# Attention with pooled keys, then a soft mixture of experts, in one planned program: the row sums' epsilon moves to ScalarE, the output gets rows of 4 KB, the groups are all of eight tiles, and the plan's places change

## The chip, the cores and the metric

The kernel runs on one core of a Trainium2 chip. The metric is the device time of one execution in microseconds (us). TensorE multiplies, VectorE and ScalarE do arithmetic and move results, GpSimd does arithmetic on the side, and SyncE issues most of the DMAs. In the profile these are PE (PEld for its weight loads), DVE, ACT, POOL and SP.

## The reference

```python
# attention: B=4, N=12288 queries, C=128; kv of 384 x 32 positions, pooled 4 x 4 to 768 keys
kv_pool = kv.reshape(B, H // r, r, W // r, r, C).mean(axis=(2, 4))
k = v = kv_pool.reshape(B, -1, C) @ w_sr
s = (q @ k.transpose(0, 2, 1)) / sqrt(C)
a = softmax(s)                       # with 1e-9 in the denominator
x = (a @ v).reshape(B * N, C)
# soft mixture: 8 experts of 4 slots, 32 slots in all
logits = x @ phi
d = exp(logits - logits.max(0)); d /= d.sum(0) + 1e-9      # over all rows
slot_out = relu(slot_input @ w1[e]) @ w2[e]                # slot_input = d.T @ x
c = exp(logits - logits.max(1)); c /= c.sum(1) + 1e-9      # over the 32 slots of a row
return c @ slot_out
```

All tensors are float32.

## The kernel before

The 49152 rows are worked on as 384 tiles of 128 queries, 96 tiles to a batch. The attention's output x is never made: since logits = a @ (v @ phi), the pooled keys times `w_sr @ phi` (called U, 32 columns) stand in for the values, and the slots' inputs are gathered over the keys first and multiplied by the values (V) once per batch.

The program has three parts.

**Head.** The first batch's kv is loaded in eight pieces of 768 KB (`kv_load0`, two halves of four pieces), added up on VectorE (`kv_pool0`, L239 to L242) and multiplied into the keys kT (`kv_k_mm` L263, `kv_k_hi` L266, `kv_k_lo` L270), U (`kv_u_mm` L278 and the steps to `kv_u_lo` L315) and V. The other batches' kv comes during the loop; GpSimd adds it up (L252).

**Loop over the tiles.** For each tile: `qk` (L353, six matmuls of the query's high and low part, which `q_hi` L340 on ScalarE and `q_lo` L343 on GpSimd split) writes the scores into one of three slots; `top` (L357, VectorE) finds the row maximum, `exp` (L369, ScalarE) the exponentials p; `hi` (L376, ScalarE) and `lo` (L379, GpSimd) split four of p's six blocks into two 16-bit halves, which a transposing DMA (`turn` L384) turns; the other two blocks are turned by TensorE (`tp` L391) and taken over by VectorE (`tev` L395). For each group of tiles: `lmm` (L411) makes the logits, `lt_out` (L432, ScalarE) and `lt_turn` (L436, TensorE) turn them back, `recip` (L444, L446) and `rcopy` (L506) prepare the softmax's sums, `logits` (L461) scales, `colmax` to `newmax` (L469 to L486) keep the running column maximum, `below`, `weights` and `scaled` (L490, L498, L511) make the weights d, `ymm` (L532, 64 matmuls for eight tiles) and `yacc` (L542) gather the slots' inputs in `acc`. `rowmax`, `rowsub` (GpSimd, L551), `rowexp` (L554) and `rownorm` (L559 to L561) make the row softmax c in the tensor LL and its reciprocal sums in RM. `lt_turn` and `rcopy` write the same PSUM bank, L; whichever stands later in the program waits for the other. At a batch's end come `yturn`, `slots` (L570, TensorE), `total` (L515 to L520) and `sacc` (L584, L585). There are 47 groups of eight tiles and two of four at the end.

**Tail.** The expert weights are loaded into buffers that the loop leaves; `t_sm` (L826), `t_h` (L842), `t_relu`, `t_ht`, `t_ho`, `t_o` (L867), `t_so`, `t_q` (L885, psq) and `t_shi`/`t_slo` make the slots' outputs shl. `k_mul` (L901, GpSimd) scales c. Then, in 24 chunks of 16 tiles: `c_t` (L908) turns c, `c_hi` (L913, ScalarE) and `c_lo` (L918, VectorE) split it, `o_mm` (L929, po) multiplies, `o_ev` (L936 on ScalarE, L938 on VectorE) takes the halves over, and `o_dma` (L942) writes each half, 512 KB.

Nothing is written in the order in which it runs. The class `Plan` takes all operations with an estimated cost, what they depend on, the buffers that they take and a priority, plays the program through, and emits an operation when its engine would take it: of those that could start within 0.12 us of the earliest, the one with the lowest priority number. A tile's or group's number is its due time plus an offset of the table `LATE`, by operation and, for the tiles' operations, by the place in the group. Each engine then runs its own instructions strictly in the emitted order.

Of the kernel before, what the change touches and what calls it, by code (L numbers as in the profile page):

```python
# [9 lines left out]
F32 = mybir.dt.float32  # L10
# [9 lines left out]
P = 128  # L20
# [99 lines left out]
def attention_then_soft_moe(ctx: ExitStack, tc: tile.TileContext, qT, kv0, kvT, w_sr, w_srT, phi, w1, w2, outT):  # L120
# [58 lines left out]
    nc.vector.memset(ones, 1.0)  # L179
    sel1 = cp.tile([P, NS], F32, tag="sel1", name="sel1")  # L180
# [50 lines left out]

    def kv_load0(h, c):
        t = kvs[h, c] = ring("p32", [P, 2, NK], F32, f"kv0_{h}_{c}").rearrange("p a b -> p (a b)")
        o = (h * R2 + c * KVC) * HK
        nc.sync.dma_start(out=t, in_=kv0[:, o : o + KVC * HK])

    def kv_pool0(h, c):
        a, v = kvs[h, 0], kvs[h, c]
        nc.vector.tensor_tensor(out=a, in0=a, in1=v, op=ALU.add)  # L239
        if c == R2 // KVC - 1:  # L240
            nc.vector.tensor_tensor(out=a[:, : 2 * HK], in0=a[:, : 2 * HK], in1=a[:, 2 * HK :], op=ALU.add)
            nc.vector.tensor_tensor(  # L242
                out=pooled[0][:, h * HK : (h + 1) * HK], in0=a[:, :HK], in1=a[:, HK : 2 * HK], op=ALU.add
            )
# [311 lines left out]
    def rownorm(g):  # L556
        s, n = groups[g]
        r = RM[:, s : s + n]
        nc.vector.tensor_reduce(out=r, in_=ll(g), axis=X, op=ALU.add)  # L559
        nc.vector.tensor_scalar_add(r, r, EPS)  # L560
        nc.vector.reciprocal(out=r, in_=r)  # L561
# [35 lines left out]
    def pool(n):  # L597
# [57 lines left out]
    def kv_ops(b, base, step, dep):  # L655
# [12 lines left out]
        p = base + step * 2  # L668
        d = dep if b else [ops["pool", 1], ops["wo"]]
# [20 lines left out]
    kv_v_ops(0, T(2), [ops["pool", 1], ops["wo"], ops["u", 0]])  # L690

    def group_ops(g):
# [46 lines left out]
        ops["c", g] = go("ks", "DVE", (0.33 * n / GMAX + 0.35, 0.1), [re_], lambda: rownorm(g))  # L739
        if (s + n) % TPB == 0:  # L740
# [4 lines left out]
            fd = go("fd", "ACT", (0.19, 0.1), [ops["nm", g], ops["to", b - 1]], lambda: fade(b, g)) if b else None  # L745
# [305 lines left out]
```

## Time and profile before

| | |
|---|---|
| timed runs | 977.13, 983.35, 1013.5 us; median 983.35 |
| profiled execution | 979.63 us; span 977.8 us |
| busy share of the span | PE 89%, DVE 82%, ACT 74%, POOL 70% |
| read and written in HBM | 58.87 MB and 25.17 MB |
| DMA packets | 452434, of them 408784 under 512 B |

The span goes from the first to the last instruction of the profiled execution. A row of the groups gives line, engine, operation, output and inputs, sizes and count, then busy time and the mean duration, then the engine's idle time before it and who ended most of it. A row of the stretches gives the busy time of PE, PEld, DVE, ACT and POOL with the number of instructions, then the granted clock of TensorE as a share of full speed, the share of the DMA engines and GB/s. A row of the timeline gives start and duration in us, engine, line, operation, and in brackets the idle time before it and what ended it.

### The profile page before, as it was taken

How to read it: one execution, taken by the hardware profiler on the slowest of the kernel's cores; microseconds unless marked ns; L12 is line 12 of the kernel's file. 1: busy time of each engine (PE TensorE's matmuls, PEld its weight loads, DVE VectorE, ACT ScalarE, POOL GpSimd, SP SyncE). 2: the span in 40 equal slices, each digit the busy share in tenths (PEclk: the TensorE clock that was granted, in tenths of full speed). 3: DMA queues.
4: the chain of work that ended last, by engine and by line, in shares of the span. 5: the costliest groups of instructions: out<-in, count | busy, mean ns of one | idle time of the engine just before them, and what ended most of it. 6: DMA issues, size and time to landing. Idle time of an engine off the chain costs nothing. (4 is left out here: it accounts for less than half of the span.)

```text
span 977.8 us, 26937 instructions
## 1 busy us (share of the span) xinstructions
PE 872.0 (89%) x10104; PEld 742.7 (76%) x10104; DVE 798.4 (82%) x1939; ACT 727.4 (74%) x1531; POOL 688.8 (70%) x584
## 2 busy tenths in 40 slices
PE   0898989999999979999998999999999999977871
PEld 0777878888888868888887989888898989753440
DVE  6687888888989898888888888889898989774761
ACT  1697868988887868887887888878888888731650
POOL 1498979776778978867688998767768787683000
PEclk9999989999999989999999999999999999987775
DMA  8499999997899998988899999888989898892999
GB/s 317 86 230 198 210 211 169 164 165 139 148 209 208 217 215 131 176 157 142 156 229 187 214 218 188 157 149 143 167 148 155 171 168 150 137 324 79 339 341 318
DMA packets 452434, 186.47 MB, mean 191 GB/s; under 512 B 408784, under 2 KB 433616, under 8 KB 452304
## 3 DMA queue, kind: packets, MB, share of 16 engines
q1 hardware_dynamic: 451728, 184.35, 92.0%
q8 instruction: 79, 1.29, 0.6%
q14 instruction: 51, 0.42, 0.2%
q10 hardware_dynamic: 576, 0.41, 0.1%
HBM read 58.87 MB, written 25.17 MB: 86 GB/s over the span
## 5 line engine op out<-in xcount | busy, mean ns | idle before, releaser
L379 POOL TENSOR_TENSOR hl<-p,hl 128x512 f16<-128x512 f32 x384 | 440.9, 1166 | 151.1 <-ACT hl L376 140.1
L353 PE MATMUL s<-kT,qs 128*128 128x384 f32 x2304 | 487.7, 352 | 6.8 <-ACT p L369 6.2
L369 ACT ACTIVATE p<-s,nm 128x768 f32<-128x768 f32 x384 | 343.9, 897 | 105.5 <-DVE nm L357 88.8
L353 PEld LDWEIGHTS s<-kT,qs 128*128 128x128 f32 x2304 | 393.0, 191 | 22.2 <-ACT p L369 18.4
L357 DVE CUSTOM_DVE_ANT_1 junk<-s,lnpk 128x768 bf16<-128x768 f32 x384 | 364.9, 950 | 26.3 <-PE s L353 10.5
L376 ACT ACTIVATE hl<-p 128x512 f16<-128x512 f32 x384 | 231.1, 626 | 7.2 <-DMA pt<-hl 3.7
L343 POOL TENSOR_TENSOR qs<-q,qs 128x512 fp32r<-128x512 f32 x96 | 123.5, 1286 | 42.3 <-ACT qs L340 31.5
L532 PE MATMUL DB<-p,dp 128*32 128x192 f32 x3040 | 135.1, 328 | 4.2 <-DVE pf L395 3.5
L395 DVE COPY pf<-DB 128x512 f32<-128x512 f32 x192 | 131.5, 685 | 4.3 <-PE DB L391 3.3
L391 PE MATMUL DB<-ident,p 128*128 128x128 f32 x768 | 117.2, 275 | 4.2 <-DVE pf L395 1.6
L532 PEld LDWEIGHTS DB<-p,dp 128*32 128x32 f32 x3040 | 96.8, 110 | 30.1 <-DVE pf L395 8.4
L391 PEld LDWEIGHTS DB<-ident,p 128*128 128x128 f32 x768 | 94.2, 141 | 15.3 <-ACT p L369 2.3
L411 PE MATMUL L<-pt,u 128*32 128x256 f16 (+1 forms) x2352 | 72.7, 271 | 3.2 <-DMA pt<-hl 3.0
L369 ACT ACTIVATION_READ_ACCUMULATOR p<-s,nm 128x1 f32 x384 | 75.0, 195 | 0.0
L411 PEld LDWEIGHTS <-u 128*32 128x32 f16 x2352 | 63.8, 97 | 12.6 <-DMA pt<-hl 3.8
L252 POOL TENSOR_TENSOR LL<-LL 128x1536 f32<-128x1536 f32 x21 | 73.2, 3486 | 0.0
L340 ACT ACTIVATE qs<-q 128x512 fp32r<-128x512 f32 x96 | 59.9, 624 | 10.5 <-DMA q<-qT 8.8
L542 DVE SCALAR_TENSOR_TENSOR acc<-acc,al,DB 128x192 f32<-128x192 f32 x44 | 18.1, 412 | 44.8 <-PE DB L532 44.8
L411 PE MATMUL L<-pf,us 128*32 128x256 f32 (+1 forms) x784 | 51.5, 380 | 2.2 <-DVE dp L511 2.0
L929 PE MATMUL po<-c,shl 32*128 32x512 f32 x288 | 37.1, 554 | 11.2 <-ACT o L936 7.5
L560 DVE TENSOR_SCALAR RM<-RM 128x8 f32<-128x8 f32 (+1 forms) x49 | 45.6, 930 | 1.7
L938 DVE COPY o<-po 128x1024 f32<-128x1024 f32 x24 | 29.3, 1221 | 19.5 <-DMA outT<-o 12.2
(135 smaller groups left out, 699.1 us busy)
## 6 DMA issues: line engine op xcount, KB each, us to landing
outT<-o SPq DMA_DIRECT2D x48, 512.0 KB, 7.5
q<-qT SPq DMA_DIRECT2D x95, 256.0 KB, 3.2
LL<-kvT SPq DMA_DIRECT2D x24, 768.0 KB, 5.1
kv<-kv SPq DMA_DIRECT2D x8, 768.0 KB, 9.6
pt<-hl SPq DMA_TRANSPOSE x384, 3.5
w<-w SPq DMA_DIRECT2D x7, 768.0 KB, 8.4
w<-w SPq DMA_DIRECT2D x11, 256.0 KB, 6.4
q<-qT ACTq DMA_DIRECT2D x1, 256.0 KB, 9.2
```

The source lines that it names most:

```text
L252: nc.gpsimd.tensor_tensor(out=stage[:, 2:4, :], in0=stage[:, 2:4, :], in1=stage[:, 0:2, :], op=ALU.add)
L340: nc.scalar.activation(QSP[i][:, 0], QS[i], AF.Copy)
L343: nc.gpsimd.tensor_tensor(out=QSP[i][:, 1], in0=QS[i], in1=QSP[i][:, 0].bitcast(F32), op=ALU.subtract)
L353: nc.tensor.matmul(s[:, h, :HK], a, k[:, m, h * HK : (h + 1) * HK], start=(n == 0), stop=(n == 2))
L357: nc.vector.tensor_tensor_reduce(out=junk.rearrange("p (h k) -> p h k", h=2), in0=S[i][:, :, :HK], in1=lnpk.unsqueeze(2).broadcast_to([P, ...
L369: nc.scalar.activation(P32[i // 2][:, i % 2, :].rearrange("p (h k) -> p h k", h=2), S.pop(i)[:, :, :HK], AF.Exp, bias=NM.pop(i), scale=1.0 ...
L376: nc.scalar.activation(HL[i][:, 0], P32[i // 2][:, i % 2, : KD * P], AF.Copy)
L379: nc.gpsimd.tensor_tensor(out=HL[i][:, 1], in0=P32[i // 2][:, i % 2, : KD * P], in1=HL[i][:, 0], op=ALU.subtract)
L391: nc.tensor.transpose(out=DB[:, o : o + P], in_=P32[u][:, h, k * P : (k + 1) * P], identity=ident)
L395: nc.vector.tensor_copy(PF[u].rearrange("p x h q -> p (x h q)"), DB[:, : 2 * KP * P])
L411: nc.tensor.matmul(out.rearrange("p (h q) -> p h q", q=P) if gt(g) == 2 else out, lhs, rhs, start=start, stop=stop)
L532: nc.tensor.matmul(G[g]["D"][j * NS : (j + 1) * NS, : NT * NS].rearrange("p (k r) -> p k r", k=NT), G[g]["dp"][:, t, :], p[:, j], start=(t ...
```

## The change

It has six parts. Lines of the changed program are some ten to twenty higher.

- **Epsilon.** `rownorm` keeps its sum alone. When a batch is done, ScalarE adds the epsilon to its 96 sums (`norm_add`) and VectorE takes the 96 reciprocals (`norm_rec`). `k_mul` waits for these.
- **Rows of the output.** The queries are laid out on the host so that within 16 tiles the tile of place 4a+b is the one that stood at 4b+a. The half of a chunk that one DMA writes is then 1024 numbers next to each other in each row of the output, where it was four runs of 256.
- **Groups.** All 48 groups have eight tiles.
- **Head.** The second half of the first kv is loaded in pieces of 4, 4, 4, 2 and 2 rows. U's products wait for the second half of the keys and get a later due time, V's too; the second query's high part waits for the second half of the keys.
- **Tail.** `c_t` waits for the last `t_h`; `t_o` does its first half for both outputs first. At a batch's end `total` stands behind `yturn`.
- **Places.** Every number of `LATE` is another, so that an engine that has a choice may take another operation first.

```diff
-        n = GMAX if NTL - at > GMAX else GMAX // 2
+        n = min(GMAX, NTL - at)
...
+    KV0 = [[4, 4, 4, 4], [4, 4, 4, 2, 2]]
...
     def rownorm(g):
         s, n = groups[g]
-        r = RM[:, s : s + n]
-        nc.vector.tensor_reduce(out=r, in_=ll(g), axis=X, op=ALU.add)
-        nc.vector.tensor_scalar_add(r, r, EPS)
+        nc.vector.tensor_reduce(out=RM[:, s : s + n], in_=ll(g), axis=X, op=ALU.add)
+
+    def norm_add(b):
+        r = RM[:, b * TPB : (b + 1) * TPB]
+        nc.scalar.activation(r, r, AF.Identity, bias=eps)
+
+    def norm_rec(b):
+        r = RM[:, b * TPB : (b + 1) * TPB]
         nc.vector.reciprocal(out=r, in_=r)
...
-        "qk": [113.0, 80.6, 90.9, 82.7, 155.0, 97.8, 116.5, 121.0],
+        "qk": [49.5, 72.6, 70.3, 44.3, 240.4, 99.2, 34.9, 65.8],
...
-        p = base + step * 2
-        d = dep if b else [ops["pool", 1], ops["wo"]]
+        p = base + step * 2 if b else T(4) + 120
+        d = dep if b else [ops["pool", 1], ops["wo"], ops["k", 0, 1]]
...
-            ops["to", b] = go("to", "DVE", (0.75, 0.1), [ya, fd], lambda: total(b, g))
...
+            ops["to", b] = go("to", "DVE", (0.75, 0.1), [ya, fd, ty], lambda: total(b, g))
+            k_ = go("na", "ACT", (0.2, 0.1), [ops["c", x] for x in range(GOF[b * TPB], g + 1)], lambda: norm_add(b))
+            ops["norm", b] = go("nr", "DVE", (0.26, 0.1), [k_], lambda: norm_rec(b))
...
-            out=outT[:, o * TS * P : (o + n) * TS * P].rearrange("p (j t q) -> p j t q", t=TS, q=P)[:, :, 2 * u : 2 * u + 2, :],
+            out=outT[:, (o * TS + 2 * u * n) * P : (o * TS + 2 * (u + 1) * n) * P],
...
-        a = op("PE", 0.2 * n, 0.3, p - 8, [KC[x] for x in need], lambda g=g: c_t(g), acq=[bk])
+        a = op("PE", 0.2 * n, 0.3, p - 8, [KC[x] for x in need] + [hx[-1]], lambda g=g: c_t(g), acq=[bk])
...
-        "qT": q.transpose(0, 2, 1),
+        "qT": q.transpose(0, 2, 1).reshape(B, C, -1, 4, 4, P).swapaxes(3, 4).reshape(B, C, NQ),
```

Three places show what this does to the order. First VectorE in a steady group (the tiles 360 to 367), from the take-over of a turned block (pf) to the scaling of the logits. Before:

```order
L395 COPY pf_12863<-DB 128x512
L559 TENSOR_REDUCE RM<-LL 128x8
L560 TENSOR_SCALAR RM<-RM 128x8
L561 RECIPROCAL RM<-RM 128x8
L444 TENSOR_SCALAR L_12813<-sums_12427 128x8
L446 RECIPROCAL r_12908<-L_12813 128x8
L506 COPY L_12813<-r_12908 128x8
L542 SCALAR_TENSOR_TENSOR acc<-acc,al_12764,DB 128x192
```

Now:

```order
L405 COPY pf_12788<-DB 128x512
L568 TENSOR_REDUCE RM<-LL 128x8
L454 TENSOR_SCALAR L_12737<-sums_12354 128x8
L456 RECIPROCAL r_12833<-L_12737 128x8
L516 COPY L_12737<-r_12833 128x8
L552 SCALAR_TENSOR_TENSOR acc<-acc,al_12689,DB 128x192
```

The add and the reciprocal on RM are gone from ahead of `recip` and `rcopy`; the rest stands as it did.

Second VectorE at the end of the loop, from the last `yacc` to `t_sm`. Before:

```order
L542 SCALAR_TENSOR_TENSOR acc<-acc,al_13778,D_13804 128x192
L515 TENSOR_REDUCE es_13834<-acc 128x1
L517 SCALAR_TENSOR_TENSOR EA<-EA,be,es_13834 128x1
L520 COPY CB<-c_13761 128x1
L564 STREAM_TRANSPOSE yt<-acc 128x192
L918 TENSOR_TENSOR c_13844<-ct_13827,c_13844 128x512
L918 TENSOR_TENSOR c_13851<-DB,c_13851 128x512
L834 TENSOR_SCALAR tsum<-pe 128x1
L835 RECIPROCAL tsum<-tsum 128x1
L584 TENSOR_TENSOR SA<-SA,dab 128x32
L585 TENSOR_TENSOR SA<-DB,SA 128x32
L826 COPY sm<-SA 128x4x4 x2
```

Now:

```order
L552 SCALAR_TENSOR_TENSOR acc<-acc,al_13571,D_13587 128x192
L579 STREAM_TRANSPOSE yt<-acc 128x192
L525 TENSOR_REDUCE es_13634<-acc 128x1
L527 SCALAR_TENSOR_TENSOR EA<-EA,be,es_13634 128x1
L530 COPY CB<-c_13565 128x1
L599 TENSOR_TENSOR SA<-SA,dab 128x32
L600 TENSOR_TENSOR SA<-DB,SA 128x32
L846 COPY sm<-SA 128x4x4 x2
```

`yturn` (yt) has gone ahead of `total` (es, EA, CB), and the two `c_lo` (L918) have left the place between it and `sacc`.

Third TensorE from the last product of `t_o` (pso) to the first of the output (po). Before:

```order
L867 MATMUL pso_13956<-w_9_13889,hT 32x512
L867 MATMUL pso_13956<-w_11_13905,hT 32x512
L885 MATMUL psq<-so,sel 128x128
L929 MATMUL po_0_13980<-c_13765,shl 128x512 x2
L929 MATMUL po_1_13982<-c_13765,shl 128x512 x2
```

Now:

```order
L887 MATMUL pso_13733<-w_9_13689,hT 32x512
L887 MATMUL pso_13733<-w_11_13699,hT 32x512
L928 MATMUL DB<-ident,LL 128x128 x4
L928 MATMUL ct_13760<-ident,LL 128x128 x4
L905 MATMUL psq<-so,sel 128x128
L928 MATMUL DB<-ident,LL 128x128 x4
L928 MATMUL ct_13780<-ident,LL 128x128 x4
L949 MATMUL po_0_13788<-c_13722,shl 128x512 x2
L949 MATMUL po_1_13790<-c_13722,shl 128x512 x2
```

Four groups of `c_t`, which used to be done before, stand now between the experts and the output; the two behind psq take banks that a `c_lo` has to leave first.

More of the change, by code (lines that the diff above doesn't have):

```diff
@@ L228, in attention_then_soft_moe, with fold @@
     kvs = {}
+    KV0 = [[4, 4, 4, 4], [4, 4, 4, 2, 2]]
     def kv_load0(h, c):
         t = kvs[h, c] = ring("p32", [P, 2, NK], F32, f"kv0_{h}_{c}").rearrange("p a b -> p (a b)")
-        o = (h * R2 + c * KVC) * HK
-        nc.sync.dma_start(out=t, in_=kv0[:, o : o + KVC * HK])
+        o = (h * R2 + sum(KV0[h][:c])) * HK
+        n = KV0[h][c] * HK
+        nc.sync.dma_start(out=t[:, :n], in_=kv0[:, o : o + n])
     def kv_pool0(h, c):
         a, v = kvs[h, 0], kvs[h, c]
[L239 to L244, printed above, removed]
+        def fold(n, out):
+            nc.vector.tensor_tensor(out=out, in0=a[:, : n * HK], in1=a[:, n * HK : 2 * n * HK], op=ALU.add)
+        n = KV0[h][c] * HK
+        nc.vector.tensor_tensor(out=a[:, :n], in0=a[:, :n], in1=v[:, :n], op=ALU.add)
+        last = c == len(KV0[h]) - 1
+        w = KV0[h][c]
+        while w > (1 if last else KV0[h][c + 1]):
+            w //= 2
+            fold(w, pooled[0][:, h * HK : (h + 1) * HK] if w == 1 else a[:, : w * HK])
     stage = LL[:, NTL - TPB :, :].rearrange("p t s -> p (t s)").rearrange("p (a b) -> p a b", a=KVC)
@@ L630, in attention_then_soft_moe @@
     for h in range(2):
-        for c in range(R2 // KVC):
+        for c, n in enumerate(KV0[h]):
             ld = op("SP", 0.3, 0.0, -300, [ld], lambda h=h, c=c: kv_load0(h, c), acq=[("p32", ("kv", h, c))])
-            land += 2.1
-            ops["land", h, c] = ld
+            land += 2.1 * n / 4
             if c:
+                last = c == len(KV0[h]) - 1
+                cost = dve(n * HK)
+                while n > (1 if last else KV0[h][c + 1]):
+                    n //= 2
+                    cost += dve(n * HK)
                 pl = op(
-                    "DVE", dve(4 * HK) + (dve(2 * HK) + dve(HK) if c == R2 // KVC - 1 else 0), 0.1, -200, [ld, pl],
-                    lambda h=h, c=c: kv_pool0(h, c), at=land,
-                    use=[("p32", ("kv", h, c))] + ([("p32", ("kv", h, 0))] if c == 1 else []),
+                    "DVE", cost, 0.1, -200, [ld, pl], lambda h=h, c=c: kv_pool0(h, c), at=land,
+                    use=[("p32", ("kv", h, c))] + ([("p32", ("kv", h, 0))] if last else []),
                 )
@@ L738, in group_ops @@
         re_ = go("re", "ACT", dv(0.31, 0.1), [rm], lambda: rowexp(g))
[L739 removed]
+        ops["c", g] = go("ks", "DVE", dv(0.33), [re_], lambda: rownorm(g))
         if (s + n) % TPB == 0:
@@ L762, in attention_then_soft_moe @@
                 if n < NB:
-                    a = op("ACT", 0.54, 0.1, t + LATE["qh"][(4 * n - groups[GOF[4 * n]][0]) // 4] if n else -50, [ops["q", n], ops.get(("ql", n - 1))], lambda n=n: q_hi(n), acq=[("qs", n)], use=[("q", n)])
+                    a = op("ACT", 0.54, 0.1, t + LATE["qh"][(4 * n - groups[GOF[4 * n]][0]) // 4] if n else -50, [ops["q", n], ops.get(("ql", n - 1)), ops["k", 0, 1] if n == 1 else None], lambda n=n: q_hi(n), acq=[("qs", n)], use=[("q", n)])
                     ops["ql", n] = op("POOL", 1.24, 0.02, t + LATE["ql"][(4 * n - groups[GOF[4 * n]][0]) // 4] if n else -50, [a], lambda n=n: q_lo(n), use=[("qs", n), ("q", n)])
@@ L985, in attention_then_soft_moe @@
     for h in range(2):
+        a = tail("PE", 0.9, ho[:2] + wl2 + ([a] if a else []), lambda h=h: t_o(h, 0), acq=[("s", ("pso", h))], use=w2k, raw=0.0)
+    for h in range(2):
         sk = ("s", ("pso", h))
-        a = tail("PE", 0.9, ho[:2] + wl2 + ([a] if a else []), lambda h=h: t_o(h, 0), acq=[sk], use=w2k, raw=0.0)
         a = tail("PE", 0.9, [a] + ho[2:], lambda h=h: t_o(h, HF), use=[sk] + w2k, raw=0.0)
```

32 lines of the change are left out of this document (17 added, 15 removed), and 8 rows, old and new, of the table LATE.

## The prediction

> **What bounds the kernel now.** The head of the page first. The profiled execution took 979.63 us, 1.83 us more than its span; the median of the three timed runs is 983.35 us, 3.7 us higher, and the sum below is made against the 979.63.
>
> ```profile
> span 977.8 us, 26937 instructions
> PE 872.0 (89%) x10104; PEld 742.7 (76%) x10104; DVE 798.4 (82%) x1939; ACT 727.4 (74%) x1531; POOL 688.8 (70%) x584
> ```
>
> 89% is a mean over three stages, so next come the sums of stretches: the loop over the tiles, and the writing of the output.
>
> ```profile
> 30.00:862.00 832.00, 790.58 (x9418) 694.49 (x9419) 720.25 (x1813) 681.87 (x1463) 662.56 (x552) 0.99 0.95 174
> 902.00:976.00 74.00, 43.77 (x334) 24.90 (x330) 38.90 (x41) 32.62 (x41) 0.00 (x0) 0.68 1.03 340
> ```
>
> In the loop (first row; PE is the first busy column, then the granted clock, the DMA share and GB/s) TensorE is busy 790.58 of 832 us and idles 41.4: it is the bound, and of this stage at most 41.4 us can go without less TensorE work. The change takes none away worth naming. In the output stage TensorE is busy 59%, but the DMA engines are full (1.03) at 340 GB/s: the transfers are the bound. So three questions remain: which of the 41.4 us go, whether the same bytes leave faster, and when the output starts.
>
> Whom did TensorE wait for? The list of waits and two lines by source:
>
> ```profile
> PE L L436 <- DVE L L506: 20.8, 11, 5.9
> L560 DVE TENSOR_SCALAR RM<-RM x49: 169/598/7581, 73.2 to 874.9; 128x8 f32<-128x8 f32 x47, 128x4 f32<-128x4 f32 x2
> L561 DVE RECIPROCAL RM<-RM x49: 178/203/206, 74.4 to 875.7; 128x8 f32<-128x8 f32 x47, 128x4 f32<-128x4 f32 x2
> ```
>
> Half of the idle time is one wait: `lt_turn` (L436) for `rcopy` (L506), 20.8 us in 11 times. And the epsilon add L560, eight numbers a partition, takes 0.169 us at its shortest and 7.581 at its longest, while the reciprocal behind it on the same tile never leaves 178 to 206 ns. The timeline puts the two together, four times:
>
> ```profile
> 125.94 5.48 DVE L560 TENSOR_SCALAR RM<-RM 128x8 f32<-128x8 f32 x1
> 132.32 0.66 PE L436 MATMUL L<-ident,lt 128*128 128x128 f32 x2 [3.76 <-DVE L L506]
> 301.94 3.08 DVE L560 TENSOR_SCALAR RM<-RM 128x8 f32<-128x8 f32 x1
> 306.77 0.41 PE L436 MATMUL L<-ident,lt 128*128 128x128 f32 x2 [2.33 <-DVE L L506]
> 353.33 2.78 PE L532 MATMUL DB<-p,dp 128*32 128x192 f32 x64
> 353.56 7.58 DVE L560 TENSOR_SCALAR RM<-RM 128x8 f32<-128x8 f32 x1
> 356.58 3.42 POOL L252 TENSOR_TENSOR LL<-LL 128x1536 f32<-128x1536 f32 x1
> 359.95 1.16 POOL L379 TENSOR_TENSOR hl<-p,hl 128x512 f16<-128x512 f32 x1
> 362.04 0.66 PE L436 MATMUL L<-ident,lt 128*128 128x128 f32 x2 [5.93 <-DVE L L506]
> 515.87 3.10 DVE L560 TENSOR_SCALAR RM<-RM 128x8 f32<-128x8 f32 x1
> 520.72 0.41 PE L436 MATMUL L<-ident,lt 128*128 128x128 f32 x2 [2.34 <-DVE L L506]
> ```
>
> The add of 353.56 ends at 361.14, 0.03 us after the last of GpSimd's instructions there, which followed each other (356.58 + 3.42, 359.95 + 1.16). VectorE stood still as long as GpSimd was at work, `rcopy` stood behind the add, and TensorE ran out of work when the 64 matmuls of `ymm` were done (356.11). I read this as the add waiting for GpSimd.
>
> **The epsilon.** 49 adds and 49 reciprocals leave VectorE; four adds on ScalarE and four reciprocals of 96 numbers come. In a steady group nothing stands between `rownorm`'s sum and `recip` any more. The four idle times are 3.76 + 2.33 + 5.93 + 2.34 = 14.4 us. Two of them also cost clock:
>
> ```profile
> 132.30:137.90 5.60, 5.58 (x20) 5.50 (x21) 3.16 (x9) 1.62 (x3) 3.81 (x3) 0.50 1.10 231
> 362.00:366.60 4.60, 4.56 (x17) 4.50 (x18) 2.99 (x8) 0.94 (x2) 0.00 (x0) 0.50 1.00 251
> ```
>
> The granted clock is 0.50 for 5.60 and 4.60 us after the two longest; at most half of that, 5.1 us, was lost. So 14.4 is the visible part and 19.5 the upper end; the lower end is 0, if another VectorE instruction meets the same GpSimd work and waits instead. I take 16: the idle time whole, since nothing else on the bounding engine can use it, and a third of the clock, as after a long stop the other engines have to refill. Late next is the rest of that list's first row, 6.4 us in seven waits, which I leave. The added wait: the reciprocal of a whole batch waits on VectorE for ScalarE's add, which stands behind one exponential; behind it stands the update of `acc`, which frees the bank for TensorE's transposes.
>
> ```profile
> L369 ACT ACTIVATE p<-s,nm 128x768 f32<-128x768 f32 x384 | 343.9, 897 | 105.5 <-DVE nm L357 88.8
> ```
>
> That is 0.9 us at three batch ends, 2.7 us if nothing hides it, nothing if the turn and the scores that stand ahead of the transposes do; `rcopy` stands before it, so `lt_turn` does not wait. I take 0.
>
> **The head, -2.** The last loads are cut in two, the scores of the first tile go ahead of the products for U, and the second query's split waits for the keys.
>
> ```profile
> 10.06 1.75 DVE L239 TENSOR_TENSOR kv<-kv,kv 128x1536 f32<-128x1536 f32 x1
> 19.28 4.62 DVE L239 TENSOR_TENSOR kv<-kv,kv 128x1536 f32<-128x1536 f32 x2
> 21.02 1.26 POOL L343 TENSOR_TENSOR qs<-q,qs 128x512 fp32r<-128x512 f32 x1 [7.68 <-ACT qs L340]
> 26.98 2.61 PE L278 MATMUL pu<-w_sb,LL 128*128 128x32 f32 x12
> 27.75 0.56 DVE L270 SCALAR_TENSOR_TENSOR kT<-pk,kT 128x384 fp32r<-128x384 f32 x1 [2.27 <-ACT kT L266]
> 29.40 3.59 PE L353 MATMUL s<-kT,qs 128*128 128x384 f32 x12
> ```
>
> Two adds took 4.62 us where one takes 1.75: 1.1 us lie beside the query's split on GpSimd, which moves away. The keys were ready at 28.31 and the scores began at 29.40, behind U's products: 1.1 us more. The smaller pieces save nothing by themselves, since VectorE adds the same numbers. Ends: 0, if the late U is then missed, and -4.
>
> **The end of the loop, -2.5.** One group of eight replaces two of four, and the transposes `c_t` may no longer slip in before the experts.
>
> ```profile
> 871.15 2.23 PE L532 MATMUL DB<-p,dp 128*32 128x192 f32 x32 [0.63 <-DVE c L918]
> 875.01 2.79 PE L532 MATMUL D<-p,dp 128*32 128x192 f32 x32
> 878.70 1.02 DVE L517 SCALAR_TENSOR_TENSOR EA<-EA,be,es 128x1 f32<-128x1 f32 x1
> 880.00 0.65 DVE L918 TENSOR_TENSOR c<-ct,c 128x512 fp32r<-128x512 f32 x1
> 880.58 0.67 DVE L918 TENSOR_TENSOR c<-DB,c 128x512 fp32r<-128x512 f32 x1
> 881.30 2.14 PE L570 MATMUL DB<-yt,v 128*128 128x32 f32 x12 [0.21 <-DVE c L918]
> 885.83 5.12 PE L842 MATMUL ph<-w,sm 128*32 128x512 f32 x32 [0.62 <-DVE sm L826]
> 898.70 1.76 PE L929 MATMUL po<-c,shl 32*128 32x512 f32 x14 [0.46 <-ACT shl L889]
> ```
>
> The sums start 3.86 us apart for the two halves; now there is one chain, with 2.2 to 2.8 us more matmuls in it: -1.5. Between the last of them (877.80) and `slots` (881.30) VectorE did `total` (1.02 us for EA alone) and two `c_lo` (1.3); now `yturn` stands first and the rest beside `slots`: -2.5. Against that, between `psq` and the first `po` stand now two groups of transposes, each of which waits for a `c_lo` (0.7): +1.5. Ends: -5 and +2.
>
> **The output, -11.** The bytes are the same, 25.17 MB, in rows of 4 KB instead of 1. What a longer row is worth, the profile shows in other transfers: the key loads of the head have rows of 6 KB.
>
> ```profile
> DMA packets 452434, 186.47 MB, mean 191 GB/s; under 512 B 408784, under 2 KB 433616, under 8 KB 452304
> 5.00:20.00 15.00, 2.26 (x4) 1.01 (x4) 11.39 (x12) 1.21 (x3) 1.26 (x1) 1.00 1.02 412
> 901.18 1.65 PE L929 MATMUL po<-c,shl 32*128 32x512 f32 x12 [0.73 <-ACT o L936]
> 903.95 1.65 PE L929 MATMUL po<-c,shl 32*128 32x512 f32 x12 [1.11 <-ACT o L936]
> ```
>
> Of the packets, 24832 lie between 512 B and 2 KB, and 25.17 MB in rows of 1 KB are 24576: one packet for each row. With all 16 engines full, 1 KB takes 16 x 1024 / 340 = 48 ns and 6 KB 16 x 6144 / 412 = 239: 38 ns a KB and 10 a packet. 4 KB then take 162 ns, 404 GB/s, and 25.17 MB take 62.3 us instead of 74.0: -11.7. Does the making keep up? One chunk of 1.05 MB follows the other by 2.77 us at half clock (901.18, 903.95), where the new rate would take one each 2.6: some 0.7 us lost until the clock rises. -11; ends 0 and -14, which is 420 GB/s, since the 412 are a mean with shorter rows in it.
>
> A rule of the Trainium skill speaks against this term: "DMA: Bandwidth & Descriptors", section "Specifications", limits a core's transfers with HBM to about 358 GB/s. By it the output takes 70.3 us, the term is -4 and the sum 955. The head's 412 GB/s do not keep to it, but they are reads, and the trace shows no write above 340.
>
> **The sum:** 979.63 - 16 - 2 - 2.5 - 11 = 948.1. The other places of the table I cost at nothing: in a steady group TensorE's instructions stand as before but for one score that changes sides with a transpose.
>
> **Rivals.** (1) Writes have a ceiling of their own, and rows of 4 KB leave at 340 to 358 GB/s. For it: only reads are seen faster. Against: the engines themselves are full at 1.03, which is what a fixed cost of each packet looks like; a ceiling behind them would look the same, so this one is not small. With none of the 11 us, 959; with a third, 955. (2) The stall changes its place: GpSimd's work stays, and VectorE's next instruction that takes its data from SBUF waits for it. Against: reciprocal and sum on the same tiles never did. Time 948 + 16 = 964. (3) Slower: in a steady group ScalarE now splits a tile (`hi`) and the next queries (`q_hi`, as many numbers) ahead of the sixth exponential, which frees a score slot.
>
> ```profile
> L376 ACT ACTIVATE hl<-p 128x512 f16<-128x512 f32 x384 | 231.1, 626 | 7.2 <-DMA pt<-hl 3.7
> ```
>
> It comes twice 0.626 us later; in 48 groups up to 60 us, 1008 us in all. It decides from 31.5 / 48 = 0.7 us a group that TensorE cannot cover. Against: before that slot is needed, TensorE does the logits and the 2.78 us of `ymm`. (4) The change does not do what it says: the rows are still cut to 1 KB. Against: the built transfers are of 1024 numbers a partition. Time 959.
>
> **Chances.** Forecast 0.58, (1) 0.18, (2) 0.13, (3) 0.06, (4) 0.02, the rest 0.03. Best ends of all terms: 979.6 - 42.5 = 937, the lower end; the upper one takes in (2) with part of (1): 968. Two per cent, which is about what a measurement of this kernel can tell from no change, is 960 against the profiled run: the forecast and most of (1) lie below, (2) within, (3) above. Faster 0.76, same 0.18, slower 0.06.
>
> **What would show it.** `lt_turn`'s wait for `rcopy` falls from 20.8 us to under 8, and TensorE's idle time in the loop from 41 to about 26; no granted clock of 0.50 inside the loop; the output stage runs at 400 GB/s, and of the 24832 packets between 512 B and 2 KB some 256 are left; the scores start near 27 us, the first `po` some 20 us earlier than 898.7. Wrong would make it a write rate that stays under 360, a VectorE instruction of several us inside the loop, or ScalarE late at the sixth exponential.

## The result: 982.5 to 929.4 us, further down than the range went

The kernel after takes 929.37 us (median of four runs, 928.39 to 934.35), the kernel before 982.51 beside it. The ratio is 0.9487, with a 95% interval of 0.9429 to 0.9544. The profiled execution of the changed kernel took 928.39 us, 51.2 less than the 979.63 from which the sum started. The forecast was 948.0, with a range of 937 to 968.

From the page of the kernel after, the head and the packets:

```profile
span 926.3 us, 26715 instructions
PE 858.6 (93%) x10038; PEld 737.7 (80%) x10038; DVE 739.9 (80%) x1832; ACT 727.9 (79%) x1531; POOL 688.5 (74%) x583
DMA packets 434145, 186.46 MB, mean 201 GB/s; under 512 B 408800, under 2 KB 409056, under 8 KB 434016
```

And its group for `lt_turn` (line, engine, operation, count, then busy time and mean, then the idle time ahead of it):

```profile
L446 PE MATMUL L<-ident,lt 128*128 128x128 f32 x96 | 20.9, 299 | 0.3
```

TensorE's idle time ahead of `lt_turn` fell from 21.0 us to 0.3, and 256 packets are left between 512 B and 2 KB. To see where the time went, the span is cut at three marks: the first exponential, the last one, the first `po`. One line's instructions have minimum, median and maximum duration, then the first and last start. The exponentials before:

```profile
L369 ACT ACTIVATE p<-s,nm x384: 882/901/912, 32.7 to 854.5; 128x768 f32<-128x768 f32 x192
```

The exponentials after, and the first products of the output:

```profile
L379 ACT ACTIVATE p<-s,nm x384: 879/897/932, 29.8 to 815.9; 128x768 f32<-128x768 f32 x192
L949 PE MATMUL po<-c,shl x288: 382/497/792, 857.1 to 914.0; 32*128 32x512 f32 x144
```

Now the sums of the stretches between the marks. The loop before:

```profile
32.70:855.40 822.70, 783.60 (x9326) 688.59 (x9324) 713.25 (x1793) 679.25 (x1458) 657.51 (x546) 0.99 0.96 176
```

After, the loop, the output, and 20 us of it:

```profile
29.80:816.80 787.00, 775.47 (x9340) 688.36 (x9339) 659.35 (x1705) 681.01 (x1463) 656.55 (x546) 1.00 0.99 184
868.00:925.00 57.00, 37.60 (x306) 21.84 (x298) 35.21 (x38) 29.21 (x37) 0.00 (x0) 0.74 0.99 393
900.00:920.00 20.00, 8.85 (x70) 4.35 (x62) 7.95 (x7) 6.18 (x7) 0.00 (x0) 0.54 1.02 406
```

| stretch | before | after | difference | forecast |
|---|---|---|---|---|
| head, to the first exponential | 32.7 | 29.8 | -2.9 | -2 |
| loop, first to last exponential | 822.7 | 787.0 | -35.7 | -16 |
| last exponential to the first `po` | 43.3 | 40.3 | -3.0 | -2.5 |
| first `po` to the end of the span | 79.1 | 69.2 | -9.9 | -11 |
| span | 977.8 | 926.3 | -51.5 | -31.5 |

The loop was forecast at less than half its size, and the other three terms came out within 1.1 us, one of them by luck, as is told further down. The loop's two rows say more: TensorE's idle time there (length less busy time) fell from 39.1 us to 11.5, and its busy time by 8.1. Part of the 8.1 is the half clock that is gone: the granted clock was 0.50 for 13.6 us of the old loop, of which at most half was lost, and never in the new one. The DMA engines are busy 0.96 of the old loop and 0.99 of the new one.

### The profile page after: what moved, and what is told of

It is laid out like the page before. It is cut to its first block, busy times and chain, and to the rows that moved or that the text cites. A ratio compares the mean times of both kernels' runs of the same rounds, so it can differ in the third digit from the quotient of the medians.

```text
span 926.3 us, 26715 instructions
## 1 busy us (share of the span) xinstructions
PE 858.6 (93%) x10038; PEld 737.7 (80%) x10038; DVE 739.9 (80%) x1832; ACT 727.9 (79%) x1531; POOL 688.5 (74%) x583
## 5 line engine op out<-in xcount | busy, mean ns | idle before, releaser
L363 PE MATMUL s<-kT,qs 128*128 128x384 f32 x2304 | 477.2, 349 | 3.2 <-ACT p L379 2.6
L421 PE MATMUL L<-pt,u 128*32 128x256 f16 x2304 | 74.5, 275 | 1.6 <-DMA pt<-hl 1.5
L421 PE MATMUL L<-pf,us 128*32 128x256 f32 x768 | 52.2, 390 | 0.3 <-DVE dp L521 0.3
L949 PE MATMUL po<-c,shl 32*128 32x512 f32 x288 | 35.1, 541 | 9.2 <-ACT o L956 8.5
L956 ACT ACTIVATE o<-po 128x1024 f32<-128x1024 f32 x24 | 24.6, 1024 | 23.3 <-PE po L949 20.8
L958 DVE COPY o<-po 128x1024 f32<-128x1024 f32 x24 | 29.3, 1220 | 10.3 <-PE po L949 10.2
```

What stands on the lines that cost most here:

```text
L363: nc.tensor.matmul(s[:, h, :HK], a, k[:, m, h * HK : (h + 1) * HK], start=(n == 0), stop=(n == 2))
L421: nc.tensor.matmul(out.rearrange("p (h q) -> p h q", q=P) if gt(g) == 2 else out, lhs, rhs, start=start, stop=stop)
L949: nc.tensor.matmul(UC[g, "po", t // 2][:, t % 2, : n * P], s[rows, a, :C], c[rows, m, : n * P], start=(k == 0), stop=(k == 2))
```

## The experiments

In all of them the loop is the stretch from the first exponential's start to the last one's end, and its row gives length, busy time of PE, PEld, DVE, ACT and POOL, clock, DMA share and GB/s. The ratio is to the kernel before on the same chip; the median of the kernel before was 978 to 986 us in these comparisons, so small differences are read from the stretches. The loop took 785.8 to 789.1 us in four kernels that plan it alike (after, and three below): a difference of 3 us in it is no evidence. With the old order times spread more: on one chip the kernel before took 970.18 to 983.29 us, even without the slowest 8 of 19 executions. Each loop below is that of one execution.

### Is it the add's wait, or the add's work?

The add back on VectorE:

```diff
-        nc.vector.tensor_reduce(out=RM[:, s : s + n], in_=ll(g), axis=X, op=ALU.add)
+        r = RM[:, s : s + n]
+        nc.vector.tensor_reduce(out=r, in_=ll(g), axis=X, op=ALU.add)
+        nc.vector.tensor_scalar_add(r, r, EPS)
+        nc.vector.reciprocal(out=r, in_=r)
```

> The kernel after with the epsilon part undone: the add and the reciprocal stand behind each group's sum on VectorE again; TensorE, GpSimd and the transfers keep their order. Theory A: 30 to 36 us more, 958 to 965, with adds of several us in the loop. Theory B: about 16 us more, 944. Theory C: less than 8 us more, below 937.

Measured: 962.52 us, ratio 0.9786 (0.9721 to 0.9852), as Theory A had it. The add's line:

```profile
L570 DVE TENSOR_SCALAR RM<-RM x48: 170/325/9376, 69.9 to 864.4; 128x8 f32<-128x8 f32 x48
```

The loop:

```profile
29.90:845.70 815.80, 780.45 (x9339) 691.69 (x9338) 708.26 (x1794) 682.04 (x1459) 656.67 (x546) 0.99 0.96 177
```

TensorE's longest row of waits in it (us in total, times, longest):

```profile
PE L L446 <- DVE L L516: 22.9, 9, 7.8
```

And the longest of the nine in the timeline:

```profile
570.15 9.38 DVE L570 TENSOR_SCALAR RM<-RM 128x8 f32<-128x8 f32 x1
570.40 2.29 POOL L389 TENSOR_TENSOR hl<-p,hl 128x512 f16<-128x512 f32 x2
572.63 1.27 POOL L353 TENSOR_TENSOR qs<-q,qs 128x512 fp32r<-128x512 f32 x1
573.86 2.27 POOL L389 TENSOR_TENSOR hl<-p,hl 128x512 f16<-128x512 f32 x2
576.08 3.42 POOL L262 TENSOR_TENSOR LL<-LL 128x1536 f32<-128x1536 f32 x1
580.43 0.66 PE L446 MATMUL L<-ident,lt 128*128 128x128 f32 x2 [7.78 <-DVE L L516]
```

The add ends at 579.53, 0.03 us after the last of GpSimd's instructions (576.08 + 3.42). The loop is 28.8 us longer: 22.9 of `lt_turn`'s wait, and 5.0 more of TensorE's busy time, at a clock of 0.99 again.

The same sum without the add's form: the epsilon stands beside each sum, and a second reduction adds the two.

```diff
+        nc.vector.tensor_reduce(out=two[:, :n, 0], in_=ll(g), axis=X, op=ALU.add)
+        nc.vector.tensor_reduce(out=r, in_=two[:, :n], axis=X, op=ALU.add)
+        nc.vector.reciprocal(out=r, in_=r)
```

> The kernel after with the epsilon again on VectorE in each group, but added by a reduction over two numbers (the sum and the epsilon beside it) instead of the add, and the reciprocal behind it. A reduction of this size never took over 0.2 us where the add did. VectorE gets 48 x 0.37 = 18 us of work back, without the wait for GpSimd. Theory A (the wait counts): 928 to 936, no instruction of several us in the loop, lt_turn's wait for rcopy under 3 us. Theory W (the work on VectorE counts, wherever it is spent): 945 to 962, like the kernel after with the add itself (962.5).

Measured: 929.29 us, ratio 0.9515 (0.9445 to 0.9585), the same as the kernel after, and Theory A again. The second reduction's line:

```profile
L572 DVE TENSOR_REDUCE RM<-two x48: 169/170/172, 68.4 to 834.1; 128x8 f32<-128x16 f32 x48
```

The loop:

```profile
29.60:815.40 785.80, 772.56 (x9337) 685.26 (x9336) 672.37 (x1794) 681.36 (x1460) 656.90 (x546) 1.00 1.00 184
```

The two kernels do the same work on VectorE at the same places (VectorE's other instructions, TensorE's, GpSimd's and the transfers keep their order). One form waits for GpSimd up to 9.4 us; the other takes 0.170 us every time. It is the wait that costs, and the 18 us of work cost nothing.

### Why the epsilon alone gives so little

The kernel before with this part alone (the number that the plan takes for the sum stays, so that the order does):

```diff
-        nc.vector.tensor_scalar_add(r, r, EPS)
-        nc.vector.reciprocal(out=r, in_=r)
...
+            k_ = go("na", "ACT", (0.2, 0.1), [ops["c", x] for x in range(GOF[b * TPB], g + 1)], lambda: norm_add(b))
+            ops["norm", b] = go("nr", "DVE", (0.26, 0.1), [k_], lambda: norm_rec(b))
```

> The kernel before with the epsilon part alone: ScalarE adds it once per batch, all else as before; TensorE, GpSimd and the transfers keep their order. The loop over the tiles became 35.7 us shorter (from the first exponential to the last: 822.7 to 787.0 us), where the prediction had 16. Theory A: it is the stalled adds, the small ones too. 49 adds took 29.3 us, where 0.169 each is 8.3: VectorE stood still for some 21 us, and with the reciprocals behind them gone as well, the loop becomes 30 to 36 us shorter and the profiled time some 945 to 950. Theory B: the four long stalls are worth what was predicted and the new table is worth the rest: 16 us less, 960 to 965. Theory C: the epsilon is worth less than 8 us, all is the table: above 971.

Measured: 969.18 us, ratio 0.9842 (0.9744 to 0.9940). The loop:

```profile
32.20:846.60 814.40, 783.70 (x9327) 691.61 (x9326) 662.92 (x1704) 681.67 (x1461) 657.78 (x546) 0.99 0.92 177
```

The two waits of TensorE that changed:

```profile
PE L L413 <- DMA pt<-hl: 14.5, 5, 4.4
PE L L438 <- DVE L L508: 2.5, 4, 0.7
```

One of the five stops in the timeline (SPq is SyncE's queue):

```profile
357.58 0.53 SPq L251 DMA_DIRECT2D LL<-kvT  x1
358.21 12.25 SPq L386 DMA_TRANSPOSE pt<-hl  x6
367.66 1.62 PE L413 MATMUL L<-pt,u 128*32 128x256 f16 x45 [4.06 <-DMA pt<-hl]
```

`lt_turn`'s wait for `rcopy` fell by 18.3 us, from 20.8 to 2.5, more than forecast. But `lmm` now waits 14.5 us for blocks that a DMA turns, where it had waited 3.0 (before), and between the two profiled executions the loop gains only 8.3. None of the theories had this second wait. How much the part is worth is less sure: by the interval of the ratio the whole gain is 6 to 25 us, so the 16 of Theory B is not excluded. Theory A also started from a wrong number: its 29.3 us are 49 times the median of 0.598. The row of the adds before has the sum:

```profile
L560 DVE TENSOR_SCALAR RM<-RM 128x8 f32<-128x8 f32 (+1 forms) x49 | 45.6, 930 | 1.7
```

At 0.169 us each they would take 8.3, so VectorE stood still for some 37 us, not 21.

The stop in the timeline ends 9.5 us after the six turning transfers began to be issued behind a 768 KB load of the next batch's kv. Two experiments ask what holds them up. First the new row of the table for `turn` alone:

```diff
-        "turn": [22.5, -4.8, -21.5, -6.7, 7.7, 32.7, -16.7, -52.3],
+        "turn": [741.8, 480.1, 722.6, 538.1, 567.9, 613.4, 689.5, 562.8],
```

> The kernel before with the epsilon part and, of the table, only the new row for turn: SyncE's queue changes its order, the other engines nearly none. With the epsilon alone lmm waited 14.5 us for turned blocks in five stops, the three longest 4.36, 4.06 and 4.14 us, each with a 768 KB load of the next kv ahead of the last turns in SyncE's queue. Theory F (the order on that queue): these waits fall under 5 us, 955 to 960. Theory G (the transfers are late for another reason: how full the DMA engines are, or what GpSimd does first): they stay above 10 us, 967 to 971.

Measured: 961.06 us, ratio 0.9834 (0.9764 to 0.9903). Loop:

```profile
32.20:838.40 806.20, 780.63 (x9327) 688.38 (x9326) 662.74 (x1704) 682.13 (x1461) 657.86 (x546) 1.00 0.92 179
```

Waits for turned blocks:

```profile
PE L L413 <- DMA pt<-hl: 8.2, 5, 4.6
```

Not quite half of the wait went, which decides for neither. So the loads themselves were made small; this kernel leaves out most of the third and fourth batch's kv, and serves for its times alone:

```diff
-        nc.sync.dma_start(out=stage[:, (2 if c == 0 else 0) : (4 if c == 0 else 2), :], in_=kvT[b - 1, :, 2 * c : 2 * c + 2, :])
+        w = NK if b == 1 else 32
+        nc.sync.dma_start(out=stage[:, (2 if c == 0 else 0) : (4 if c == 0 else 2), :w], in_=kvT[b - 1, :, 2 * c : 2 * c + 2, :w])
```

> The kernel before with the epsilon part alone, and of the next batch's kv the loads for the third and fourth batch cut to 32 of 768 columns (the keys of these two batches are then made from numbers left over from the second); adds, order and every other transfer stay. The loads for the second batch are whole, and so the stop of lmm for turned blocks near 90 us (4.36) is the control. Theory L (the bytes of a load hold up the turning transfers behind it): the stops near 364 and 572 us (4.06 and 4.14) fall under 0.5 each, the one near 90 us stays over 3, and the loop is 6 to 12 us shorter than 814.4: profiled 960 to 966. Theory M (the turns are late because GpSimd splits late, behind the adds): the stops near 364 and 572 us stay over 3 us and the time within 4 us of 972.

Measured: 951.36 us, ratio 0.9735 (0.9652 to 0.9817). Loop:

```profile
32.00:828.50 796.50, 777.51 (x9327) 686.09 (x9326) 662.16 (x1704) 681.15 (x1461) 658.12 (x546) 1.00 0.87 166
```

Waits for turned blocks:

```profile
PE L L414 <- DMA pt<-hl: 3.9, 1, 3.9
```

The one stop that is left is the control near 90 us; those near 364 and 572 us are gone, and the loop is 17.9 us shorter. GpSimd was as busy as before (658.1 and 657.8 us), and Theory L holds in all its parts but the size: the loop gained 17.9 us where it allowed 12, since the three stops that went (9.6 us) are not all: the two groups of eight tiles around the stop near 364 us went from 17.6 and 22.0 us to 16.1 each, the one at 572 us from 22.1 to 16.3. Of the 17.9 us, 2.5 lie in the first batch, where the loads are whole. So with the epsilon gone, the next thing late in the loop is the turned block, held up by the bytes of the bulk loads. Whether they hold it up in the queue or at the engines, the two runs do not separate.

It is not simply that the DMA engines are full. The stretch from 340 to 400 us has two of these loads in both programs. With the epsilon alone, and in the kernel after:

```profile
340.00:400.00 60.00, 54.29 (x614) 47.96 (x614) 45.03 (x118) 46.67 (x101) 50.82 (x42) 0.97 1.01 187
340.00:400.00 60.00, 59.62 (x731) 52.74 (x733) 50.51 (x130) 52.73 (x116) 58.44 (x47) 1.00 1.14 202
```

The DMA share is higher in the kernel after (1.14 against 1.01), and TensorE is busy 59.62 of the 60 us there, against 54.29.

### The places: worth nothing alone, much together

The new numbers of `LATE` in the kernel before, and the old ones in the kernel after: all numbers of the table but that of `total`, which is the same in both; one row is shown, one way and then the other.

```diff
-        "exp": [80.8, 5.7, 52.5, -26.2, 33.4, 31.0, 46.4, 108.6],
+        "exp": [351.5, 437.7, 308.8, 323.6, 259.2, 458.0, 225.1, 424.8],
```

> The kernel before with the new numbers of the table alone; adds and reciprocals stay on VectorE, group by group. Theory A: the new places are worth nothing by themselves: 976 to 984, and adds of several us are seen at other points of the loop, since the add still waits for GpSimd. Theory B: 16 to 20 us less, 960 to 964. Theory C: 30 us less or more, below 950.

> The kernel after with the old numbers of the table; all other parts stay. Theory A: within 4 us of the kernel after, 925 to 933. Theory B: 16 to 20 us more, 944 to 949. Theory C: 30 us more.

Measured: 994.16 us, ratio 1.0135 (1.0086 to 1.0184), and 983.61 us, ratio 1.0016 (0.9981 to 1.0050). The loop of the first:

```profile
32.80:865.80 833.00, 790.13 (x9328) 693.77 (x9327) 695.35 (x1793) 681.46 (x1458) 657.02 (x546) 0.98 0.94 173
```

TensorE's main waits in the first:

```profile
PE L L411 <- DVE dp L511: 12.0, 6, 3.1
PE L L436 <- DVE L L506: 8.3, 3, 5.9
```

The loop of the second:

```profile
29.80:871.90 842.10, 798.70 (x9340) 688.35 (x9339) 664.32 (x1705) 682.45 (x1463) 657.54 (x546) 0.99 0.93 172
```

And its main wait:

```profile
PE s L363 <- ACT p L379: 14.7, 28, 2.3
```

None of the three theories holds, though of Theory A the sign came: an add of 6.5 us at 163 us, where the kernel before has no long one. The new numbers make the old program's loop 10.3 us longer, and the old numbers make the new program's loop 55.1 us longer, which loses the whole gain. Of the 55.1, 31.9 are idle time of TensorE, in which the wait that is shown is the largest, and 23.2 are busy time, for as many instructions; how the old numbers bring this about is not settled here. The table is worth nothing or 55 us, depending on what it is combined with. The first wait of the first kernel is worth a look: `lmm` waits for `scaled` (dp), which frees the bank L. I read it as logits that stand too early in TensorE's order. Then both parts together in the kernel before, the two diffs of the epsilon and of the table that were shown, without the rest:

```diff
-        "exp": [80.8, 5.7, 52.5, -26.2, 33.4, 31.0, 46.4, 108.6],
+        "exp": [351.5, 437.7, 308.8, 323.6, 259.2, 458.0, 225.1, 424.8],
...
+            ops["norm", b] = go("nr", "DVE", (0.26, 0.1), [k_], lambda: norm_rec(b))
```

> The kernel before with the epsilon part and the new numbers of the table, nothing else. The epsilon alone took 8.3 us out of the loop (814.4), the table alone put 10.2 in (832.9), all parts together took 35.7 out (787.0). Theory D: these two parts make the loop's gain and need each other; the loop takes 785 to 793 us and the profiled time is 943 to 952. Theory E: they only add up, or the gain needs the head and the groups of eight too: the loop takes 805 to 825 us, above 962.

Measured: 979.78 us, ratio 1.0035 (1.0000 to 1.0071): no gain at all, as Theory E had it. Loop:

```profile
32.40:851.60 819.20, 782.02 (x9327) 689.81 (x9326) 657.43 (x1704) 681.22 (x1460) 656.69 (x546) 1.00 0.92 176
```

TensorE's main waits:

```profile
PE L L413 <- DVE dp L513: 12.8, 7, 2.7
PE s L355 <- ACT p L371: 9.3, 14, 2.2
```

The wait for `scaled` is there again (12.8 us). TensorE's order differs from the kernel after in the first groups and in six groups at the start of each later batch, so the batch's end was undone in the kernel after, and then added to the kernel before:

```diff
-            fd = go("fd", "ACT", (0.19, 0.1), [ops["nm", g], ops["to", b - 1]], lambda: fade(b, g)) if b else None
-            ops["to", b] = go("to", "DVE", (0.75, 0.1), [ya, fd, ty], lambda: total(b, g))
...
+            fd = go("fd", "ACT", (0.19, 0.1), [ops["nm", g], ops["to", b - 1]], lambda: fade(b, g)) if b else None
+            ops["to", b] = go("to", "DVE", (0.75, 0.1), [ya, fd], lambda: total(b, g))
             m = go("ms", "DVE", (0.35, 0.1), [ops["nm", g], ops.get(("sa", b - 1))], lambda: mstep(b, g), use=[lk])
```

> The kernel after with the operations of a batch's end planned as before: fade and total ahead of the running maximum's step, and total no longer behind yturn. With the new numbers of the table the plan then emits total some 15 places earlier on VectorE and yturn some 6 places later, sacc over 20, and TensorE's order in six groups at the start of each batch is another; everything else keeps its order. Theory H (the new places need this part): the loop gets 25 to 35 us longer, like that of the kernel before with epsilon and places (819.2), 955 to 965. Theory I (that kernel missed the head, the groups of eight or the number that the plan takes for the sum): within 4 us of 929.

Measured: 947.11 us, ratio 0.9615 (0.9560 to 0.9669). Loop:

```profile
29.90:833.30 803.40, 779.55 (x9339) 687.44 (x9338) 658.62 (x1705) 683.20 (x1463) 656.68 (x546) 1.00 0.97 180
```

TensorE's main waits:

```profile
PE s L363 <- ACT p L379: 6.6, 10, 1.7
PE L L421 <- DVE dp L521: 5.4, 5, 2.7
```

The loop is 16.4 us longer, with the same two waits. That is clearly not nothing, but under the 25 that Theory H gave. Then the same diff the other way, in the kernel before with epsilon and places, and the plan's number for the sum:

```diff
-        ops["c", g] = go("ks", "DVE", (0.33 * n / GMAX + 0.35, 0.1), [re_], lambda: rownorm(g))
+        ops["c", g] = go("ks", "DVE", dv(0.33), [re_], lambda: rownorm(g))
...
+            ops["to", b] = go("to", "DVE", (0.75, 0.1), [ya, fd, ty], lambda: total(b, g))
```

> The kernel before with the epsilon part, with the plan's number for the sum, the new numbers of the table and the new order at a batch's end; head, groups, tail and the output's rows as before. From the fifth group on TensorE's order is that of the kernel after. Theory H: the loop takes 785 to 793 us (819.2 without the batch's end), profiled 943 to 951. Theory I: above 805 us, 963 or more.

Measured: 956.90 us, ratio 0.9696 (0.9648 to 0.9744). Loop:

```profile
32.60:828.60 796.00, 776.06 (x9326) 688.37 (x9324) 659.01 (x1704) 680.21 (x1461) 656.82 (x546) 1.00 0.94 181
```

The loop came from 819.2 to 796.0, where epsilon and table alone had not gained anything to speak of: the table works only together with the new batch's end and the plan's number for the sum, which these runs do not part. It is 3 us outside Theory H's range, and the 9.0 us that are missing to 787.0 are the subject of the next run.

### The head

```diff
-    KV0 = [[4, 4, 4, 4], [4, 4, 4, 2, 2]]
+    KV0 = [[4, 4, 4, 4], [4, 4, 4, 4]]
...
-        p = base + step * 2 if b else T(4) + 120
+        p = base + step * 2
...
-    kv_v_ops(0, T(6) + 130, [ops["pool", 1], ops["wo"], ops["u", 0]])
+    kv_v_ops(0, T(2), [ops["pool", 1], ops["wo"], ops["u", 0]])
```

(and U's products and the second query's split without the keys' second half)

> The kernel after with the head as before: four equal pieces, U's and V's products early, the second query's split not held back. Only the first four groups change their order on TensorE. By the prediction's term 2 us more, with ends of 0 and 4: 929 to 933. The first stretch of 24 tiles was 4 us shorter in the kernel after than before (41.7 to 45.7): if the head makes that as well, 6 to 7 us more, 934 to 937.

Measured: 944.43 us, ratio 0.9573 (0.9530 to 0.9617). More than either expectation. Loop:

```profile
32.40:828.00 795.60, 775.67 (x9328) 689.07 (x9327) 658.62 (x1704) 680.83 (x1461) 656.57 (x546) 1.00 0.95 181
```

Two of TensorE's waits, which were 1.5 and 2.6 us in the kernel after:

```profile
PE L L421 <- DMA pt<-hl: 4.5, 6, 1.2
PE s L363 <- ACT p L379: 3.7, 8, 0.9
```

The first exponential comes 2.6 us later, and the loop is 8.6 us longer, as long as in the run before. Of these, 3.1 lie in the first batch, where the order differs. The third batch took 203.9 us here and 204.1 in the run before, and 199.8 to 200.8 in the four kernels with the new head, though every engine has the same order there; why, these runs do not settle. Another 3.0 us of the difference lie between the last exponential and the first `po` (43.3 against 40.3), a stretch that spreads by itself, as the last of these runs shows.

### The output, and the place of c_t

```diff
-            out=outT[:, (o * TS + 2 * u * n) * P : (o * TS + 2 * (u + 1) * n) * P],
+            out=outT[:, o * TS * P : (o + n) * TS * P].rearrange("p (j t q) -> p j t q", t=TS, q=P)[:, :, 2 * u : 2 * u + 2, :],
...
-        "qT": q.transpose(0, 2, 1).reshape(B, C, -1, 4, 4, P).swapaxes(3, 4).reshape(B, C, NQ),
+        "qT": q.transpose(0, 2, 1),
```

> The kernel after with the output's rows of 1 KB again (and the queries laid out as before); every engine keeps its order. If the longer rows are worth what the prediction said, 10 to 12 us more: 938 to 942, the output at 340 GB/s and 24832 packets between 512 B and 2 KB. If the gain of the tail came from its earlier start or from elsewhere, within 4 us of 929.

Measured: 942.04 us, ratio 0.9634 (0.9575 to 0.9693), 12.7 us more than the kernel after. The output:

```profile
868.00:938.00 70.00, 43.16 (x322) 24.33 (x322) 37.24 (x40) 31.20 (x40) 0.00 (x0) 0.74 1.04 340
```

The first `po`:

```profile
L949 PE MATMUL po<-c,shl x288: 382/496/792, 860.3 to 920.8; 32*128 32x512 f32 x144
```

The packets:

```profile
DMA packets 452577, 186.46 MB, mean 198 GB/s; under 512 B 408800, under 2 KB 433632, under 8 KB 452448
```

340 GB/s again, where 4 KB rows gave 405 to 406. From the first `po` to the end of the span it is 79.5 us (939.8 - 860.3) against 69.2: 10.3 us are the rows, and 2.1 of the rest are a loop that took 789.1.

```diff
-        a = op("PE", 0.2 * n, 0.3, p - 8, [KC[x] for x in need] + [hx[-1]], lambda g=g: c_t(g), acq=[bk])
+        a = op("PE", 0.2 * n, 0.3, p - 8, [KC[x] for x in need], lambda g=g: c_t(g), acq=[bk])
```

> The kernel after with c_t no longer waiting for the last t_h, so that the first transposes of c may again go ahead of the experts. By the prediction 1.5 us of the time lie between psq and the first po because of that wait: 927 to 928. If they stand where TensorE waits for other work anyway: within 1 us of 929.4, which this measurement would call the same. If they hold up the experts: 930 to 933.

Measured: 932.23 us, ratio 0.9447 (0.9403 to 0.9490). Loop:

```profile
29.80:818.60 788.80, 775.18 (x9339) 688.77 (x9339) 658.96 (x1705) 682.36 (x1463) 656.54 (x546) 1.00 1.00 183
```

The ratio's interval overlaps that of the kernel after, and of the 4.0 us more in its span (930.3) 1.8 lie in the loop, which it does not change. From the last exponential to the first `po` it takes 42.2 us where the kernel after takes 40.3. But the six other kernels with the new tail take 41.4 to 43.7 us there, and the seven with the old one 41.0 to 44.3. So no gain is seen, and 1.5 us either way can't be told in this stretch.

## Why the prediction was right and wrong

**What failed: the loop's -16.** Its mechanism was right as far as it went: the idle time ahead of `lt_turn` did go (20.8 to 0.3 us), the clock of 0.50 left the loop, and VectorE's longest instruction in it now takes 1.1 us. But the term went wrong in four ways.

1. It was too small for its own wait. It counted four of the eleven waits of `lt_turn`, 14.4 of 20.8 us, left the other seven without a reason, and took a third of 5.1 us for the clock. Between the two kernels the loop lost the 20.8 us of this wait, 6.8 us of other idle time and 8.1 us of TensorE's busy time, together the 35.7. With the add alone put back into the new program, `lt_turn` waits 22.9 us and the loop is 28.8 us longer, not 16.
2. "Nothing else on the bounding engine can use it." In the old order something took its place: with the epsilon alone, `lmm` stopped 14.5 us for turned blocks behind bulk loads, and the profiled loop gained 8.3 us. "Late next is the rest of that list's first row" named the wrong thing.
3. "The other places of the table I cost at nothing." In a steady group that was right: eight tiles took 16.1 us before and 16.0 after (from one exponential's start to the eighth next). But only about half of the groups are steady. The others also carry a batch's end, the keys, U and V, or the loads and adds of the next kv, and there the order differs. The four batches took 204.9, 213.3, 206.2 and 198.2 us before and 194.8, 198.1, 200.8 and 193.2 after. The old numbers in the new program cost 55.1 us.
4. "`yturn` first" was costed only at the program's end. It stands at three more batch ends, and with the new table the loop needs the new planning there: 16.4 us without it. And without the new head the loop is 8.6 us longer, where the term of -2 held only the way to the first exponential; 3.1 of these lie where the order differs, and the cause of the rest is open.

One way from the old loop to the new one: 822.7, with the epsilon 814.4, with the table 819.2, with the batch's end and the plan's number 796.0, with the head, the groups and the tail 787.0. The first two of these steps are no larger than the old order's spread. Taken away one at a time from the end, the add costs 28.8, the table 55.1, the batch's end 16.4 and the head 8.6: 109 us of a gain of 35.7. The parts do not add up, and no share of the gain belongs to one of them. What is shown for each is what it costs to leave it out; why the table's numbers and the batch's end need each other is not shown.

**What held.** The add waits for GpSimd, and another form of the same sum does not (929.29 against 962.52). The output's term: -9.9 for the -11 forecast. In all runs with rows of 4 KB the time from the first `po` to the end is 68.2 to 69.5 us, and in all with 1 KB 78.8 to 79.5. The rate is 405 to 406 GB/s in the middle of the output (393 over 868 to 925 us) for the 404 worked out from the price of a packet; the packets of 4 KB took 159 ns in the median, for the 162 forecast. The head up to the first exponential came out at -2.9 for -2, and this too repeats: 29.6 to 29.9 us with the new head, 32.0 to 32.8 with the old.

**What came out by luck.** The way to the first `po`, -3.0 for -2.5, rests on one execution each. Over all kernels this stretch takes 40.3 to 43.7 us with the new tail and 41.0 to 44.3 with the old, so no gain there is shown, and none of the three terms in it.

**The rivals.** As for the rule that was weighed, the limit of about 358 GB/s of the Trainium skill ("DMA: Bandwidth & Descriptors", section "Specifications"): the writes of this kernel ran at 406, so for them the measurement decides against it. The same page's section "Bandwidth" says that each core gets about 358 GB/s where both cores of an HBM domain stream; one core was at work here. Rival (1) falls with the 406.

Rival (2), the stall at another place, happened in a form that was not foreseen: not on VectorE, but in the transfers, and in the old order. In the kernel after, TensorE's waits for turned blocks and for exponentials are short:

```profile
PE L L421 <- DMA pt<-hl: 1.5, 2, 1.3
PE s L363 <- ACT p L379: 2.6, 5, 0.9
```

(3), ScalarE late at the sixth exponential, did not come: TensorE waits 2.6 us for exponentials in all, where it had waited 6.2 (before). (4) fell with the packets.

## What to carry to other kernels

Before costing a removed wait, count all of its occurrences, and ask what the same engine will wait for next in the same place: here it was blocks turned by a DMA behind a bulk load. A full column alone does not tell it: at a DMA share of 1.01 the loop stopped for these blocks, and at 1.14, in another order, it did not. In a program whose order comes from a plan, a table of places is fitted to the operations around it; its effect is measured with and without the other parts, since a part alone can give nothing, and the steady group tells nothing about the groups that carry side work. A term that comes out right in one execution is worth checking against the same stretch of the other runs. And a tiny instruction whose maximum is fifty times its minimum is worth another form: here a reduction over two numbers in place of an add with a constant.

## What the runs showed of the hardware

In these runs the form of a VectorE instruction decides whether it waits for GpSimd. The add of a constant to 128x8 numbers, read from SBUF and written to it, took 0.170 to 9.376 us and ended, where it was longest, 0.03 us after a chain of GpSimd instructions, six of which began while it stood. A reduction from 128x16 to 128x8 at the same place took 0.169 to 0.172 us, and the reciprocal of 128x8 behind it 0.203 to 0.204, through the same GpSimd work. An add of a constant that reads SBUF and writes PSUM (L454, 128x8, in the kernel after) took 0.158 to 0.172 us in 48 cases, at another place. The wait can last over several instructions in a row, not only to the end of the one that runs. The Trainium skill ("SBUF — State Buffer", section "SBUF: two separate sides") has VectorE and GpSimd share a port pair: a GpSimd instruction, or a VectorE instruction in a two-port mode or with two inputs in SBUF, holds it for the whole instruction, and the other blocks. That the add waits agrees with it if the add ran in such a mode, which no run here shows; the wait over six instructions is what this trace adds.

Writes of 4 KB rows left at 405 to 406 GB/s with the engines full (1.02), and of 1 KB rows at 340 (1.04), in two kernels that differ only in the layout of queries and output. A packet of 1 KB took 48 ns and one of 4 KB 159, in the median.
